# A spectral filter and a feed-forward block on one core: contiguous PSUM writes in the channel stage, ScalarE interleaving even and odd, an evacuation split by bank, table work and statistics in another order

## The chip, the cores and the metric

The kernel runs on one core of one Trainium2 chip. The metric is the device time of one execution in microseconds (us). Before the change it was 194.46 us, the median of three runs (193.75, 194.46 and 197.01). The engines are called as the profile calls them: PE is TensorE (PEld its weight loads), DVE is VectorE, ACT is ScalarE, POOL is GpSimd and SP is SyncE.

## The reference, cut to what matters

```python
x = A_x                                   # 1 x 2048 x 512, bf16
h = x + _A_ref(_layernorm(x), A_w_r, A_w_i)
h2 = h + _B_ref(_layernorm(h), B_w1, B_b1, B_w2, B_b2)

def _A_ref(x, w_r, w_i):
    X = rfft2(x.astype(float32)) * (w_r + 1j * w_i)     # 2048 x 257 frequencies
    return irfft2(X, s=(2048, 512)).astype(bfloat16)

def _B_ref(x, w1, b1, w2, b2):                          # 512 -> 1792 -> 512
    h = relu(x @ w1 + b1)
    return (h * h) @ w2 + b2
```

## The kernel before, in words

Both transforms are made of matmuls against sine tables. The 2048 rows lie as 128 partitions by 16 groups `g`; the 2048-point transform is split in two factors, and the 512-point transform over the channels is split into even and odd frequencies. The order of every engine's instructions is the order in which the kernel is written: at the end `pin` chains all instructions of an engine (L22 to L31, called in L610). Four stretches follow each other.

**Head.** POOL writes integer angle tables (`idxL` and `fiG` for the channel table GF, `idxK` and `fiE` for the row tables EF), ACT turns them into sines. DVE takes the statistics of each group of x (L195 and L196; the groups 3, 7, 11 and 15 are summed by ACT in L188 and L189), POOL makes 1/sqrt of the variance (L203, L204), DVE normalizes (L208). `stage1(g0)` (L211) multiplies two groups by the small table KF and ACT writes them to `Bt` (L222). PE also transposes EF into EI (L264, L270), which DVE copies out of PSUM (L272).

**Channel and row stages, a loop over eight pairs `pr`.** `stage2(pr)` (L309) is the channel transform: eight matmuls of 128x256 into a PSUM tile `p2`, whose even and odd columns lie interleaved (`r j e`), so that a matmul for one `e` writes every second fp32. ACT copies the tile to `U` in bf16 (L318). `stage3(pr)` (L320) multiplies U by the row table EF (L338 to L341) and ACT copies the result to `AB` (L343). `spectral(pr)` (L355) is DVE work: the butterfly that makes X of the next pair out of AB (L352, L353), the products with the weights (L361, mA and mB), Z (L371, L372) and M (L381, L383), while POOL does the real frequencies (L297 to L304). `stage4(pr)` (L386) is the inverse row transform (L399, L400); ACT copies its tile to `T2` (L408), and for the last pair the copy is cut into three pieces on ACT, DVE and ACT (L404 to L406). The PE order in one turn is stage3(pr+2), stage2(pr+3), stage4(pr-1).

**Boundary.** `s5` multiplies T2 by the inverse channel table GI (L455), ACT copies the odd half (L458), `s5b` adds and subtracts (L464, L465), `s6` is the last small transform plus the residual (L469, L470), `s6b` the statistics of the second layer norm (L474, L475), `rstd` and `norm` finish it (L478, L479, L494), `transp` transposes (L506). For the first chunk of two groups this is written out by hand (L591 to L607), with matmuls on ones (`warm`, L227) between.

**Feed-forward.** Five chunks of groups; `up` (L544, L547, L548) and `down` (L563, L567) of one chunk run with the boundary steps of the next chunk between them (`prep_steps`, L514).

## Time and profile before

| what | value |
|---|---|
| runs | 193.75, 194.46, 197.01 us; median 194.46 |
| the profiled execution's own time | 193.75 us |
| its span in the profile | 192.0 us |
| busy: PE / DVE / ACT / POOL | 166.8 / 129.1 / 97.3 / 57.1 us |
| mean granted clock of PE | 0.982 |

The span is the time from the first to the last recorded instruction; the time of the execution holds 1.75 us more. A busy PE is not a PE at its peak: a matmul of 128x256 counts as busy with 270 to 420 ns though the next one begins 110 or 217 ns after it. The chain of waits follows the end of the program back through what released each step. A group's line has the line number, the engine, the operation, tiles and shapes, the count, then busy us and mean ns, then the idle time just before.

### The profile page before, as it was taken

Reading aid. Unit: us, or ns where it says so; the run is one execution under the profiler, and the core shown is the slowest. Engines: PE = TensorE matmul, PEld = TensorE weight load, DVE = VectorE, ACT = ScalarE, POOL = GpSimd, SP = SyncE. Lnnn points to the kernel's source line nnn. Section 1 sums busy time; section 2 is a strip of 40 time slices with the busy share of each in tenths; the row PEclk is TensorE's granted clock in tenths of the full one; section 3 lists DMA queues with packets and bytes.
Section 4 is the critical chain, followed back from the end, with each engine's and each line's share of the span. In section 5 each row is a group of like instructions: output and inputs, shape, how many; then the busy total and the mean of one; then the engine's idle time right before and its main releaser. Section 6 shows DMA issues by size and latency. Waiting matters only on the chain.

```text
span 192.0 us, 2699 instructions
## 1 busy us (share of the span) xinstructions
PE 166.8 (87%) x946; PEld 91.3 (48%) x946; DVE 129.1 (67%) x308; ACT 97.3 (51%) x152; POOL 57.1 (30%) x117
## 2 busy tenths in 40 slices
PE   6667987799864867889999989999999999999992
PEld 2235754366532426744654344544455444456540
DVE  7899717878876174994699724899445986448421
ACT  3499747476783205723774146771327760338400
POOL 8977614543153012302240202240202422006000
PEclk9979999999999699999999999999999999999999
DMA  6857999600000000000000000000100000010001
GB/s 178 301 103 112 296 372 363 139 3 3 0 2 0 0 0 3 0 0 29 27 3 0 27 27 27 3 0 0 55 27 31 2 0 27 27 60 0 0 29 53
DMA packets 13323, 11.19 MB, mean 58 GB/s; under 512 B 2302, under 2 KB 12158, under 8 KB 13310
## 3 DMA queue, kind: packets, MB, share of 16 engines
q1 hardware_dynamic: 13310, 11.03, 20.0%
q8 instruction: 7, 0.11, 0.3%
q14 instruction: 6, 0.05, 0.1%
HBM read 8.93 MB, written 3.02 MB: 62 GB/s over the span
## 4 chain that ended last, share of the span: by engine, by line
PE 59%; DVE 23%; ACT 9%; POOL 5%; issue 2%; ACTq 0%; POOLq 0%; DVEq 0%
PE ph L544 19%; PE po L563 19%; PE p L315 7%; DVE act L548 4%; ACT U L318 4%; DVE st L474 3%; DVE hs L470 3%; DVE st L195 3%; PE p L455 3%; DVE un L208 2%; PE p L506 2%; DVE R L464 2%; DVE R L465 2%; POOL rs L479 1%; ACT u L491 1%
## 5 line engine op out<-in xcount | busy, mean ns | idle before, releaser
L547 ACT ACTIVATE rl<-ph,b1f 128x384 bf16<-128x384 f32 (+2 forms) x70 | 41.9, 602 | 23.7 <-PE ph L544 22.0
L544 PE MATMUL ph<-UT,W 128*128 128x384 bf16 (+2 forms) x280 | 52.9, 336 | 0.5 <-ACT UT L510 0.5
L563 PE MATMUL po<-W,act 128*128 128x512 bf16 x224 | 50.8, 379 | 0.0
L548 DVE TENSOR_TENSOR act<-rl 128x384 bf16<-128x384 bf16 (+2 forms) x70 | 32.3, 478 | 13.0 <-ACT rl L547 12.7
L544 PEld LDWEIGHTS <-W 128*128 128x128 bf16 x280 | 27.4, 98 | 20.1 <-issue 0.6
L551 POOL TENSOR_TENSOR hb<-hs,b2b 128x512 f32<-128x512 bf16 x16 | 18.4, 1152 | 57.2 <-DVE act L548 57.2
L563 PEld LDWEIGHTS <-act 128*128 128x128 bf16 x224 | 21.6, 98 | 26.9 <-issue 2.7
L567 DVE TENSOR_TENSOR ot<-po,hb 128x512 bf16<-128x512 f32 x16 | 11.0, 689 | 18.4 <-PE po L563 18.4
L491 ACT ACTIVATE u<-hs,nm,rs 128x512 bf16<-128x512 bf16 x6 | 4.7, 808 | 24.5 <-DVE nm L488 24.5
L315 PE MATMUL p<-GF,Bt 128*128 128x256 bf16 x64 | 15.0, 417 | 1.0 <-ACT Bt L222 1.0
L219 PE MATMUL p<-KF,un 128*128 128x256 bf16 x32 | 8.0, 290 | 4.8 <-DVE un L208 4.8
L478 POOL TENSOR_SCALAR rs<-mv 128x3 f32<-128x3 f32 (+2 forms) x5 | 1.2, 239 | 35.3 <-DVE mv L475 35.3
L318 ACT CAST U<-p 128x1024 bf16<-128x1024 f32 x8 | 8.1, 1012 | 6.9 <-PE p L315 6.9
L315 PEld LDWEIGHTS <-Bt 128*128 128x128 bf16 x64 | 8.2, 130 | 6.4 <-ACT Bt L222 1.1
L470 DVE SCALAR_TENSOR_TENSOR hs<-p,xs 128x512 bf16<-128x512 f32 x16 | 10.8, 678 | 0.6 <-PE p L469 0.5
L474 DVE BATCH_NORM_STATS2 st<-hs 128x6 f32<-128x512 bf16 x16 | 11.0, 686 | 0.2
L455 PE MATMUL p<-GI,T 128*128 128x256 bf16 x64 | 10.3, 291 | 0.0
L227 PE MATMUL p<-ones 128*128 128x512 bf16 x25 | 8.7, 497 | 1.4 <-DVE ones L139 1.4
L510 ACT COPY UT<-p 128x768 bf16<-128x768 bf16 (+2 forms) x5 | 4.2, 842 | 10.5 <-PE p L506 10.5
L399 PE MATMUL p<-EI,M 128*128 128x256 bf16 x28 | 6.9, 278 | 2.8 <-DVE M L381 1.9
L469 PE MATMUL p<-R,KI 128*128 128x512 bf16 x16 | 6.1, 380 | 3.4 <-DVE R L465 3.2
L227 PEld LDWEIGHTS <-ones 128*128 128x128 bf16 x43 | 4.8, 116 | 8.7 <-issue 5.1
(134 smaller groups left out, 232.2 us busy)
## 6 DMA issues: line engine op xcount, KB each, us to landing
W<-in_B_w_dram SPq DMA_DIRECT2D x2, 1792.0 KB
out_dram<-ot SPq DMA_DIRECT2D x16, 128.0 KB, 1.8
xs<-in_A_x_dram SPq DMA_DIRECT2D x3, 512.0 KB, 6.5
WB<-Wrev SPq DMA_DIRECT2D x2, 449.8 KB, 6.4
WB<-in_A_w_r_dram SPq DMA_DIRECT2D x1, 514.0 KB, 11.9
WB<-in_A_w_i_dram SPq DMA_DIRECT2D x1, 514.0 KB, 7.2
xs<-in_A_x_dram SPq DMA_DIRECT2D x2, 256.0 KB, 3.5
Wrev<-in_A_w_r_dram SPq DMA_DIRECT2D x1, 449.8 KB
```

What stands on the lines that cost most here:

```text
L227: nc.tensor.matmul(o, lhsT=ones[:, 0:P], rhs=ones[:], start=True, stop=True)
L315: nc.tensor.matmul(puv[:, q, :, e, :], lhsT=Bt[:, 2 * t + e, 2 * pr + q, :], rhs=GFv[:, t, :, e, :], start=(t == 0), stop=(t == 1))
L318: nc.scalar.copy(U[:].rearrange("p q c -> p (q c)"), pu[:])
L455: nc.tensor.matmul(pe[:, 256 * e:256 * e + 256], lhsT=T2[:, g, lt].rearrange("p q s -> p (q s)"), rhs=GI[:, lt, :], start=(r == 0), stop=( ...
L470: nc.vector.scalar_tensor_tensor(hs[:, g, :], py[:], WSC, xs[:, g, :], ALU.mult, ALU.add)
L474: nc.vector.bn_stats(st[:], hs[:, g, :])
L544: nc.tensor.matmul(ph[:, 0:n], lhsT=W1[:, d, bass.ts(f, P)], rhs=UT[:, d, 0:n], start=(d == 0), stop=(d == ND - 1))
L547: nc.scalar.activation(rl[:, 0:n], ph[:, 0:n], ACT.Relu, bias=b1f[:, f:f + 1], scale=1.0)
L548: sq = nc.vector.tensor_tensor(act[:, f, 0:n], rl[:, 0:n], rl[:, 0:n], ALU.mult)
L551: add = nc.gpsimd.tensor_tensor(hb[:, g, :], hs[:, g, :], b2b[:], ALU.add)
L563: nc.tensor.matmul(po[:], lhsT=act[:, f, bass.ts(i, P)], rhs=W2[:, f, :], start=(f == 0), stop=(f == NF - 1))
L567: nc.vector.tensor_tensor(ot[:], po[:], hb[:, g, :], ALU.add)
```

## The change

- The PSUM tile of stage2 has the order `q r e j`: the even columns stand together, then the odd ones, each in runs of 128. The ACT copy to U puts them back in the order `r j e`, writing every second bf16.
- T2 has `lt` outside and `g` inside. stage4 takes its four parts in the order 1, 0, 3, 2 instead of 1, 3, 0, 2, so that the first two lie in the first bank of the tile. The last pair's copy is in two pieces, ACT for the first bank and DVE for the second.
- Table work: the row tables (`idxK`, `fiE`) come first on POOL, those for GF after the second batch's statistics; the negation of EF on DVE and `idxD` on POOL come after stage1.
- Statistics: in the head `bn_aggr` of a group is issued after `bn_stats` of the next. In every chunk the first group's statistics of the second layer norm are taken by ACT (a Copy and a Square pass with accumulators) instead of DVE, and POOL makes the variance out of them with two more small operations.
- Order on PE: the transposes of EF come before stage1(8), and three matmuls on ones ahead of it are gone; four stand after the transposes into `tr2`, five in each turn of the loop from pr = 5 on. At the boundary s5(0) and s5(1) come first, then three on ones; both s5b come ahead of s6(0).

```diff
     def stage2(pr):
         pu = mm_tile("p2")
-        puv = pu[:].rearrange("p (q r j e) -> p q r e j", q=2, r=2, e=2)
+        puv = pu[:].rearrange("p (q r e j) -> p q r e j", q=2, r=2, e=2)
...
-        nc.scalar.copy(U[:].rearrange("p q c -> p (q c)"), pu[:])
+        nc.scalar.copy(U[:].rearrange("p q (r j e) -> p (q r) e j", r=2, e=2),
+                       pu[:].rearrange("p (q r e j) -> p (q r) e j", q=2, r=2, e=2))
...
-        for lt in (1, 3, 0, 2):
+        for lt in (1, 0, 3, 2):
...
-        src = pt[:].rearrange("p (l q g s) -> p g l q s", l=4, q=2, g=G)
+        src = pt[:].rearrange("p (l q g s) -> p l g q s", l=4, q=2, g=G)
         if split:
             nc.scalar.copy(dst[:, 0:2], src[:, 0:2])
-            nc.vector.tensor_copy(dst[:, 2:9], src[:, 2:9])
-            nc.scalar.copy(dst[:, 9:16], src[:, 9:16])
+            nc.vector.tensor_copy(dst[:, 2:4], src[:, 2:4])
...
+        if pr >= 5:
+            warm(mm_tile("idle")[:, 0:512], 5)
...
     def ln1_stats(a, b):
-        for g in range(a, b):
-            if g not in ON_ACT:
-                st = fwd.tile([P, 6], FP32, tag="st", bufs=4, name="st")
+        mine = [g for g in range(a, b) if g not in ON_ACT]
+        sts = {}
+        for k in range(len(mine) + 1):
+            if k < len(mine):
+                g = mine[k]
+                sts[g] = st = fwd.tile([P, 6], FP32, tag="st", bufs=4, name="st")
                 nc.vector.bn_stats(st[:], xs[:, g, :])
-                nc.vector.bn_aggr(mv1[:, g, :], st[:])
+            if k > 0:
+                g = mine[k - 1]
+                nc.vector.bn_aggr(mv1[:, g, :], sts.pop(g)[:])
...
+    def s6b(g, on_act=False):
+        if on_act:
+            for f, sc, k in ((ACT.Copy, 1.0 / D, 0), (ACT.Square, float(D) ** -0.5, 1)):
+                junk = ffn.tile([P, D], BF16, tag="junk", bufs=2, name="junk")
+                nc.scalar.activation(junk[:], hs[:, g, :], f, scale=sc, accum_out=mv2[:, g, k:k + 1])
...
+    def rstd(a, b, on_act=()):
+        for g in on_act:
+            nc.gpsimd.tensor_tensor(nm2[:, g:g + 1], mv2[:, g, 0:1], mv2[:, g, 0:1], ALU.mult)
+            nc.gpsimd.tensor_tensor(mv2[:, g, 1:2], mv2[:, g, 1:2], nm2[:, g:g + 1], ALU.subtract)
...
-            steps.append(lambda g=g: s6b(g))
-        steps.append(lambda: rstd(a, b))
+            steps.append(lambda g=g: s6b(g, g == a))
+        steps.append(lambda: rstd(a, b, (a,)))
...
+    s5(0)
+    s5(1)
     idle = bank("idle", "ph", 3)
     warm(idle[:], 3)
-    s5(0)
-    s5(1)
     s5b(0)
-    warm(idle[:], 2)
+    s5b(1)
     s6(0)
-    s5b(1)
-    s6b(0)
-    warm(idle[:], 2)
+    s6b(0, True)
     s6(1)
     s6b(1)
-    rstd(0, 2)
+    rstd(0, 2, (0,))
     norm(0, False)
-    warm(idle[:], 11)
+    warm(idle[:], 14)
```

The order of instructions moves at three places that matter below. Line numbers of the changed kernel are its own. First POOL in the head, from the small index tables on (`idxL` and `fiG` feed GF, `idxK` and `fiE` feed EF, `rs` is 1/sqrt of the variance). Before:

```order
L147 MEMSET mhalf 128x4
L148 IOTA idxL 128x512
L150 MEMSET idxL 128x1
L172 TENSOR_SCALAR fiG<-idxL,cols 128x257
L173 TENSOR_SCALAR fiG<-idxL,cols 128x255
L172 TENSOR_SCALAR fiG<-idxL,cols 128x257
L173 TENSOR_SCALAR fiG<-idxL,cols 128x255
L175 IOTA idxK 128x1152
L203 TENSOR_SCALAR rs_87<-mv_86 128x2
L204 TENSOR_TENSOR rs_87<-rs_87,mhalf 128x2
```

With the change:

```order
L147 MEMSET mhalf 128x4
L167 IOTA idxK 128x1152
L170 TENSOR_SCALAR fiE_123<-idxK,cols 128x1152
L200 TENSOR_SCALAR rs_87<-mv_86 128x2
L201 TENSOR_TENSOR rs_87<-rs_87,mhalf 128x2
L170 TENSOR_SCALAR fiE_124<-idxK,cols 128x1152
L198 TENSOR_TENSOR nm_88<-mv_86 128x1
```

The second `fiE` now stands right behind the first `rs`, which DVE's first normalization waits for; the four `fiG` have moved behind the `rs` of the groups 4 to 7, which the normalization of these groups waits for.

Second the end of the loop on DVE, with the waits: the last M, the copy of the last stage4 tile to T2 and the first s5b. With the change:

```order
L389 TENSOR_TENSOR M<-Z 128x512 [waits DVE_49,PE_49,Pool_49]
L391 TENSOR_TENSOR M<-Z 128x512
L413 CAST T_69<-p_794 128x32x16 [waits Activation_49]
L473 TENSOR_TENSOR R<-p_825,od 128x256 [waits Activation_49]
L474 TENSOR_TENSOR R<-p_825,od 128x256
```

The copy of the second bank (L413) waits on ACT's semaphore, for the count that ACT's copy of the first bank brings it to; and that ACT copy waits for PE's count after all eight matmuls of the tile. Before, the copy on DVE (L405) waited for ACT in the same way.

Third PE at the boundary, from the last stage4 matmul of the loop (L400, in the changed kernel L408) to the first s5 (L455, now L464). Before:

```order
L400 MATMUL p_775<-EI,M 128x256
L227 LDWEIGHTS ones
L227 MATMUL idle<-ones 128x512 [waits Activation_49]
L227 LDWEIGHTS ones
L227 MATMUL idle<-ones 128x512
L227 LDWEIGHTS ones
L227 MATMUL idle<-ones 128x512
L455 LDWEIGHTS T_69
L455 MATMUL p_805<-GI,T_69 128x256
```

With the change:

```order
L408 MATMUL p_794<-EI,M 128x256
L224 LDWEIGHTS ones
L224 MATMUL idle<-ones 128x512 [waits PE_49]
L224 LDWEIGHTS ones
L224 MATMUL idle<-ones 128x512
L224 LDWEIGHTS ones
L224 MATMUL idle<-ones 128x512
L224 LDWEIGHTS ones
L224 MATMUL idle<-ones 128x512
L224 LDWEIGHTS ones
L224 MATMUL idle<-ones 128x512
L464 LDWEIGHTS T_69 [waits DVE_49,Activation_49]
```

Before, three matmuls on ones stood ahead of the first s5 and waited for ACT's last copy to T2 (L406), because their bank was that tile's. Now five stand there that wait for nothing but PE itself, and the wait for the copies to T2 is on the weight load of s5. Behind the eight matmuls of s5 follow three on ones and then both s6 (L478).

More of the change, by code (lines that the diff above doesn't have):

```diff
@@ L77 @@
     GI = persist.tile([P, 4, 256], BF16, name="GI")
-    T2 = persist.tile([P, G, 4, 16, 8], BF16, name="T2")
+    T2 = persist.tile([P, 4, G, 16, 8], BF16, name="T2")
     fwd = tc.alloc_tile_pool(name="fwd", bufs=1)
@@ L244 @@
     stage1(2, 4)
-    nc.vector.tensor_scalar(EF[:, :, 2, :], EF[:, :, 0, :], -1.0, None, ALU.mult)
     nc.gpsimd.memset(ident[:], 0.0)
@@ L258 @@
     ln1_norm(8, 12)
-    stage1(8, 3)
+    stage1(8)
     stage1(10)
-    tr = mm_tile("ptr", BF16)
-    for j in range(16):
-        nc.tensor.transpose(tr[:, P * j:P * j + P], EF[:, j // 2, j % 2, :], ident[:])
     ln1_norm(12, 16)
```

46 lines of the change are left out of this document (25 added, 21 removed).

## The prediction

> **What bounds the kernel now.** I read the stages first: busy time by stretch, cut where the chain of waits changes its character (columns: stretch, length, then busy us of PE, PEld, DVE, ACT and POOL, granted clock, DMA).
>
> ```profile
> 0.00:24.70 24.70, 17.51 (x109) 10.38 (x110) 21.06 (x59) 17.58 (x29) 18.66 (x49) 0.93 0.79 201
> 24.70:61.60 36.90, 30.26 (x172) 18.29 (x173) 26.15 (x63) 23.55 (x25) 14.29 (x42) 1.00 0.35 109
> 61.60:74.00 12.40, 7.96 (x37) 3.71 (x37) 6.13 (x14) 2.12 (x5) 0.97 (x2) 0.86 0.00 0
> 74.00:192.00 118.00, 111.09 (x630) 58.89 (x629) 75.71 (x172) 54.03 (x94) 23.20 (x24) 1.00 0.06 19
> ```
>
> Head (DVE busiest), loop over pairs (no engine full), boundary (nobody busy), feed-forward (PE 94%). Then the chain of waits through one turn of the loop (start us, us, what):
>
> ```profile
> 42.09 1.74 PE p L315 x8
> 43.91 1.02 ACT U L318
> 44.97 0.38 PE p L338
> ...
> 46.00 1.74 PE p L315 x8
> ```
>
> The turn is a circle PE – ACT – PE: eight matmuls of stage2, their copy to U, stage3 on U, the next stage2. 3.91 us a turn. The groups by shape tell what is odd in it:
>
> ```profile
> L315 PE MATMUL p<-GF,Bt 128*128 128x256 bf16 x64 | 15.0, 417 | 1.0 <-ACT Bt L222 1.0
> L219 PE MATMUL p<-KF,un 128*128 128x256 bf16 x32 | 8.0, 290 | 4.8 <-DVE un L208 4.8
> L318 ACT CAST U<-p 128x1024 bf16<-128x1024 f32 x8 | 8.1, 1012 | 6.9 <-PE p L315 6.9
> L343 ACT CAST AB<-p 128x1024 bf16<-128x1024 f32 x7 | 7.1, 1013 | 3.4 <-PE p L341 3.4
> L121 ACT ACTIVATE GF<-fiG 128x1024 bf16<-128x1024 int16 x1 | 1.0, 1039 | 0.0
> ```
>
> L315 and L219 stream the same 256 columns with new weights each time. L315 writes every second fp32 of PSUM and takes 1.74/8 = 0.217 us from start to start at full clock. L219 writes two runs of 128:
>
> ```profile
> 18.93 0.11 PE p L219
> ```
>
> So the interleaved write costs stage2 twice the time: 0.87 us a turn.
>
> DVE has slack in that circle, but little. Its rows (start, us, tile; the bracket is the wait before):
>
> ```profile
> 30.30 0.69 DVE L361 TENSOR_TENSOR mA<-X,WB 128x1024 bf16<-128x1024 bf16 x1 [0.87 <-ACT X L334]
> ...
> 53.27 0.69 DVE L361 TENSOR_TENSOR mA<-X,WB 128x1024 bf16<-128x1024 bf16 x1
> ...
> 55.54 0.43 DVE L352 TENSOR_TENSOR X<-AB 128x512 bf16<-128x512 bf16 x1 [0.98 <-ACT AB L343]
> ...
> 57.56 0.68 DVE L361 TENSOR_TENSOR mA<-X,WB 128x1024 bf16<-128x1024 bf16 x1
> ...
> 60.14 0.42 DVE L383 TENSOR_TENSOR M<-Z 128x512 bf16<-128x512 bf16 x1
> ```
>
> A turn of DVE is 57.56 − 53.27 = 4.29, less 0.98 of waiting: 3.31 us. That is the next bound.
>
> **Loop: what the change takes.** Stage2 becomes 8 × 0.109 = 0.87. Its copy to U reads runs of 128 and writes every second bf16. No ACT row writes so; the nearest in kind is the sine of GF, which reads every second int16 and takes 1039 ns against 1012 to 1013 of the copies. Low bound 1.01; high bound twice that, 2.02, by what a step of two costs PE's writes to PSUM. I take 1.02, since the row on the same engine is the nearer one. The circle is then 3.91 − 0.87 = 3.04 us, shorter than DVE's 3.31. ACT has three copies a turn (AB, U, T2), 3 × 1.01: also shorter. So DVE sets the turn, and the gain is not 0.87 a turn but about 0.6.
>
> From DVE's first product to its last M is now 60.56 − 30.30 = 30.26 us. Without waits it is 7 × 3.31 + 3.00 (the last turn, from 57.56, without a butterfly) = 26.2: **−4.1**. The start gains more: stage3(0) stands on PE behind both first stage2, 3.5 us. With 1.74 us for the two, it waits for the first U instead: 0.87 + 0.2 (drain and semaphore) + 1.02 = 2.1, about **−1.3**. Loop **−5.4** in all; bounds −6.2 (if the turn is 3.2) and +0.6 (copies at 2.02: a circle of 4.04, seven times 0.13 over 3.91, and −0.3 at the start). What DVE now waits for first if I am wrong is AB (the wait of L352).
>
> **Boundary.** The chain from DVE's last M to the first matmul of the feed-forward:
>
> ```profile
> 61.59 0.28 ACT T L404
> ...
> 61.89 0.64 DVE T L405
> ...
> 62.55 0.54 ACT T L406
> ...
> 63.13 1.44 PE idle L227 x3
> 64.57 0.87 PE p L455 x4
> ...
> 68.57 0.61 DVE st L474
> ...
> 69.38 0.59 DVE hs L470
> ...
> 73.98 1.03 PE ph L544 x8
> PEclk9979999999999699999999999999999999999999
> ```
>
> Copies: three in a row end 2.5 us after M (60.56). In the new order ACT still waits for all eight matmuls and DVE for ACT. Two pieces of 512 elements are by estimate 0.6 (0.54 for 448) and 0.7 (0.64 for 448): 1.3 against 1.5. But the second part of stage4 (lt 0 instead of lt 3) now waits for POOL's real sums, which come after M; by the lead of one part's two matmuls, 0.2, I set that off. I count 0 for the split.
> The three matmuls on ones, 1.44 us, leave the path: **−1.4**. Five others take their place and end, at half of 1.44/3 each at full clock, 1.2 us after stage4, under the 1.3 us of copies; without that cover they would cost 1.2. The clock digit of the 14th slice (62.4 to 67.2) is 6, and s5 ran at 0.87/4 = 0.217 a matmul; with PE kept busy it runs at 0.11: **−0.4**.
> Statistics: the chain holds hs, st and mv twice. Now DVE does R twice, hs twice, one st; ACT takes the first group in the shadow of the second hs. Its cost has rows in the head:
>
> ```profile
> 5.07 0.63 ACT L188 ACTIVATE un<-xs 128x512 bf16<-128x512 bf16 x1 [2.55 <-DMA xs<-in_A_x_dram]
> ...
> 6.35 0.19 ACT L189 ACTIVATION_READ_ACCUMULATOR un<-xs 128x1 f32 x1
> ```
>
> 6.54 − 5.07 = 1.47 us, against hs (0.6), st and mv (0.8) of the second group on DVE: level, so st and mv of the first group, 0.8, go, and R of the second group now fills the time in which s6(0), a matmul of 512 columns (0.38 as in L338), runs; POOL's added subtraction I put at 0.2 behind it. **−1.0**. Boundary **−2.8**, bounds −3.3 and −1.4 (only the matmuls on ones).
>
> **Head.** DVE's rows, and the POOL row that lies over one of them:
>
> ```profile
> 8.46 0.66 DVE L195 BATCH_NORM_STATS2 st<-xs 128x6 f32<-128x512 bf16 x1
> ...
> 9.26 0.66 DVE L195 BATCH_NORM_STATS2 st<-xs 128x6 f32<-128x512 bf16 x1
> ...
> 10.05 1.58 DVE L208 TENSOR_SCALAR un<-xs,mv,rs 128x512 bf16<-128x512 bf16 x2
> 11.55 0.48 DVE L245 TENSOR_SCALAR EF<-EF 128x1152 bf16<-128x1152 bf16 x1
> ...
> 19.82 1.79 DVE L208 TENSOR_SCALAR un<-xs,mv,rs 128x512 bf16<-128x512 bf16 x4 [0.37 <-POOL rs L204]
> ```
> ```profile
> 3.32 0.49 POOL L173 TENSOR_SCALAR fiG<-idxL,cols 128x255 int32<-128x255 int32 x1
> ...
> 8.62 2.55 POOL L178 TENSOR_SCALAR fiE<-idxK,cols 128x1152 int32<-128x1152 int32 x2
> ```
> ```profile
> L208 DVE TENSOR_SCALAR un<-xs,mv,rs x16: 381/408/1260, 7.0 to 21.0; 128x512 bf16<-128x512 bf16 x16
> ```
>
> A statistic with its aggregation costs 0.80 from start to start, and the aggregation has to wait until the 0.66 are through; with another statistic between I take 0.70, for twelve less the last of each batch: −0.8. The negation of EF leaves DVE's path to Bt: −0.4. The normalization at 10.05 took 1.58 for two where 0.75 is usual; its first instruction, 1260 ns, ended when POOL's fiE did. This goes (−0.8) and comes back at two places: the second fiE now starts together with the first normalization (I take +0.6, half of its length), and the four fiG lie over that of the groups 4 to 7 (+0.4, what the row at 19.82 shows, where POOL writes fiI: 1.79 for four against 1.4). Net +0.2. On PE the 16 transposes no longer stand between stage1(10) and stage1(12): from the last normalization (19.82 + 1.79 = 21.6) to stage2(0) (24.7, the cut of the stretches) 3.1 us pass, where the last four matmuls (0.4), drain and semaphores (0.4) and a copy (1.0) need 1.8: −1.3. Stage2(0) now also waits for DVE's negation of EF (0.4) and its copy of the transposes out of PSUM (2048 elements against the negation's 1152; by estimate 0.9 at its rate, 1.2 with PSUM as the source), 1.6 behind the last normalization: just covered, and 0.1 to 0.5 if not. Sum −0.8 − 0.4 + 0.2 − 1.3 = −2.3, of which I take **−2.1**; bounds −3.3 (no overlap with POOL) and 0 (1.2 for fiE and 4 × 0.49 for fiG, each blocking DVE to its end).
> The upper bound is what a rule of the Trainium skill gives, "SBUF — State Buffer", section "Who interferes with whom", by which a DVE copy or tensor_scalar in a two-port mode and POOL exclude each other, and whoever issues first keeps the shared ports for the whole instruction. The 1260 ns instruction agrees; the 1.79 for four, with four POOL instructions beside them, does not go that far.
>
> **Feed-forward.** Per chunk DVE loses 0.8 us and ACT gains 1.47.
>
> ```profile
> 73.90:91.40 17.50, 15.62 (x112) 10.32 (x112) 12.03 (x35) 8.99 (x20) 3.42 (x4) 1.00 0.03 9
> 91.40:115.30 23.90, 22.70 (x136) 12.29 (x134) 17.13 (x41) 11.72 (x21) 4.74 (x5) 1.00 0.05 17
> ```
>
> PE idles 1.9 and 1.2 us in the first two chunks, behind DVE; later PE is full and nothing is to be had. Behind ACT's two passes are queued the relus of the next columns, for which PE's `up` waits with three buffers. I take **−0.4**; bounds −1.5 and +1.5 (one pass uncovered in each of two chunks, less a little).
>
> **Sum**, against the profiled execution's 193.75 us (span 192.0): −5.4 − 2.8 − 2.1 − 0.4 = −10.7, so 183.05. That execution is 0.7 below the median, and the fastest of three; I put little of this on it and predict **183.2 us**, against a median of 194.46 before.
>
> **Rivals.** (1) The loop gets only half: DVE goes on waiting for AB, because ACT's three copies, which fill 3.04 of 3.31 us, queue behind each other and GI's sine once more. For it speaks the 0.98 us in the row quoted, a turn in which that sine stands ahead of AB; against it the 0.27 us of slack that each other turn gains. Then 183.2 + 2.7 = 185.9. Chance 0.18.
> (2) The head gains nothing, because each fiE and fiG blocks a normalization to its end: 183.2 + 2.1 = 185.3. For it the 1260 ns row, against it the row at 19.82, where four POOL instructions beside four normalizations cost only 0.4. Chance 0.12. The rule of the Trainium skill quoted above leads here.
> (3) U at twice the time: loop +0.6 instead of −5.4, 189.2. For it: PE's own writes at a step of two. Chance 0.05.
> (4) Slower: the copy writing every second bf16 is no longer a matter of 1 ns an element. The circle is then 2.02 us plus the copy c, on the path seven times and once at the start: 7 × (2.02 + c − 3.91) + (c − 1.02 − 1.3). It decides from where this is +5.3, what the rest gains: c = 2.6 us. At 3.04, three times the row, it is +8.8 and the time 197.4. Nothing in the trace is that slow at a step of two. Chance 0.03.
> That the split is not a split (DVE waits for ACT) is already in the sum.
>
> **Chances and range.** The forecast, 180.3 to 185.0, has 0.62; (1) and (2) 0.30, (3) 0.05, (4) 0.03. The range 179.6 to 187.5 holds the forecast, (1) and (2), and below it the lower bounds of loop and boundary together. A measurement tells about 2% (3.9 us) from no change, so faster means below 190.6: 0.93, with most of (3); within 2%: 0.04; slower 0.03.
>
> **What would show it.** Right: L325, the new line of L315, from start to start at 0.109 us; U near 1.02 us; DVE without a wait before X from the third pair on, turn 3.2 to 3.4; the first s5 some 2.5 us after the last M; full clock there; stage2(0) near 22.6; the feed-forward near 117.6 us. Wrong: U above 1.2 us, AB waits on DVE over 0.3 us a turn, normalizations above 1 us more than twice, or PE idling more than before in the first chunks.

## The result and the profile after

The changed kernel takes 187.3 us (median of four runs, 187.29 to 187.33) against 195.7 of the kernel before in the same session (four runs, 193.75 to 197.01). The ratio, 0.965 with a 95% interval of 0.962 to 0.968, so faster by 3.5%, is taken over the quicker runs of before (193.75 and 194.46) alone, since 196.89 and 197.01 belong to a slower kind that this kernel shows in every session. Forecast were 183.2 us and a gain of 10.7; in the profiled executions the gain is 6.4 (193.75 to 187.33), and the span falls by 6.5, from 192.0 to 185.5. So the direction is right and 4.2 us of the sum are missing. The time lies outside the forecast's own interval, 180.3 to 185.0, and 0.2 us inside the wider range that took in rivals (1) and (2).

The stages again, cut at the same events (the first stage2, the last M, the first matmul of the feed-forward; columns as before: stretch, length, busy us of PE, PEld, DVE, ACT, POOL, granted clock, DMA):

```profile
0.00:24.20 24.20, 17.19 (x108) 9.87 (x109) 20.99 (x57) 17.80 (x29) 18.68 (x49) 1.00 0.78 194
24.20:56.00 31.80, 25.23 (x177) 16.63 (x180) 26.53 (x66) 25.10 (x24) 14.73 (x42) 1.00 0.44 135
56.00:66.30 10.30, 8.29 (x46) 4.08 (x48) 5.32 (x12) 3.25 (x8) 1.59 (x6) 1.00 0.00 0
66.30:185.50 119.20, 111.07 (x621) 58.88 (x629) 73.13 (x165) 57.49 (x110) 25.16 (x32) 1.00 0.06 18
```

| stretch | before | after | measured | forecast |
|---|---|---|---|---|
| to the first stage2 (24.68, 24.23) | 24.7 | 24.2 | −0.45 | −2.1 |
| to the last M (60.56, 55.98) | 35.9 | 31.75 | −4.1 | −5.4 |
| to the feed-forward's first matmul (73.98, 66.31) | 13.4 | 10.3 | −3.1 | −2.8 |
| to the end | 118.0 | 119.2 | +1.2 | −0.4 |

**The loop.** The groups by shape (busy us, then mean ns of one):

```profile
L325 ACT CAST U<-p 128x1024 bf16<-128x1024 f32 x8 | 10.3, 1307 | 1.1 <-PE p L322 1.1
L322 PE MATMUL p<-GF,Bt 128*128 128x256 bf16 x64 | 8.1, 273 | 0.1
L351 ACT CAST AB<-p 128x1024 bf16<-128x1024 f32 x7 | 7.1, 1014 | 3.4 <-PE p L349 3.3
```

Stage2's group falls from 15.0 us and 417 ns to 8.1 and 273, close to L219 before (290 ns): the contiguous write does what was forecast. But the copy to U, now with a step of two on its write, takes 1307 ns against 1014 of AB's copy beside it. In the chain of waits through one turn (start us, us, what) the two copies stand one behind the other:

```profile
37.85 0.38 PE p L346
38.28 0.38 PE p L348
38.66 0.23 PE p L349
39.04 0.76 ACT AB L351
39.95 1.32 ACT U L325
41.31 0.38 PE p L346
```

41.31 − 37.85 = 3.46 us a turn. Stage3 of one pair, its AB, then the U of the next pair, which stands behind AB on ACT, then the next stage3: that is the circle, 0.24 longer than DVE's own turn (3.22, as the kernels without these waits show further down). DVE waits for AB in the last four of its seven turns with a butterfly, 0.16 to 0.18 us and once 0.64, where the sine of GI stands ahead of AB on ACT (columns: start, us, engine, line; the wait in brackets):

```profile
43.55 0.43 DVE L360 TENSOR_TENSOR X<-AB 128x512 bf16<-128x512 bf16 x1 [0.16 <-ACT AB L351]
...
50.95 0.42 DVE L360 TENSOR_TENSOR X<-AB 128x512 bf16<-128x512 bf16 x1 [0.64 <-ACT AB L351]
```

**The boundary.** The chain after the last M (55.56 + 0.42 = 55.98), and PE's granted clock over the span in 40 slices:

```profile
57.07 0.59 ACT T L412
57.69 0.70 DVE T L413
58.53 0.61 PE p L464 x4
...
61.66 1.34 ACT junk L485 x4
```
```profile
PEclk9999999999999999999999999999999999999998
```

The two copies come one after the other, as forecast; s5 starts 2.55 us behind M (4.01 before) and the slice that showed a 6 is at 9. ACT's sums are now a step of the chain.

**The head.** DVE's rows after, and three of DVE before for the same work:

```profile
2.08 1.12 DVE L157 TENSOR_SCALAR mask<-subc,pF 128x128 bf16<-128x128 int32 x1
...
3.75 1.18 DVE L166 TENSOR_SCALAR KF<-KF 128x128 bf16<-128x128 bf16 x1
4.84 1.27 DVE L190 BATCH_NORM_STATS2 st<-xs 128x6 f32<-128x512 bf16 x2
...
7.50 1.57 DVE L205 TENSOR_SCALAR un<-xs,mv,rs 128x512 bf16<-128x512 bf16 x2 [0.37 <-POOL rs L201]
...
13.73 2.05 DVE L205 TENSOR_SCALAR un<-xs,mv,rs 128x512 bf16<-128x512 bf16 x4
...
18.52 1.38 DVE L205 TENSOR_SCALAR un<-xs,mv,rs 128x512 bf16<-128x512 bf16 x4 [0.67 <-POOL rs L201]
20.51 1.64 DVE L205 TENSOR_SCALAR un<-xs,mv,rs 128x512 bf16<-128x512 bf16 x4 [0.61 <-POOL rs L201]
```
```profile
2.09 0.57 DVE L160 TENSOR_SCALAR mask<-subc,pF 128x128 bf16<-128x128 int32 x1
...
3.44 0.42 DVE L169 TENSOR_SCALAR KF<-KF 128x128 bf16<-128x128 bf16 x1
3.81 0.70 DVE L195 BATCH_NORM_STATS2 st<-xs 128x6 f32<-128x512 bf16 x1
```

And POOL after, at the same times:

```profile
2.01 1.11 POOL L167 IOTA idxK<- 128x1152 int32 x1
3.65 1.23 POOL L170 TENSOR_SCALAR fiE<-idxK,cols 128x1152 int32<-128x1152 int32 x1 [0.53 <-DVE cols L163]
...
17.44 1.04 POOL L201 TENSOR_TENSOR rs<-rs,mhalf 128x4 f32<-128x4 f32 x1
...
19.43 1.05 POOL L201 TENSOR_TENSOR rs<-rs,mhalf 128x4 f32<-128x4 f32 x1
```

Lay the two over each other. The mask, 0.57 before, ends at 3.20, just behind the idxK row (3.12); the sign change of KF, 0.42 before, ends at 4.93, just behind the first fiE (4.88). Before, POOL did shorter pieces there, and the same two instructions ended just behind these: the mask at 2.66 behind idxL (2.59), the sign change at 3.86 behind a fiG (3.81). The first statistic is 1.03 us later for it, before any of the forecast's gains begins. At the end DVE waits twice for rs, 0.67 and 0.61, with its statistics long done: POOL, which now has idxL and the four fiG ahead of these rs, has become the head's bound.

**The feed-forward.** ACT, DVE and PE in the first chunk (three answers of the timeline):

```profile
72.15 0.62 ACT L485 ACTIVATE junk<-hs 128x512 bf16<-128x512 bf16 x1
...
73.38 0.46 ACT L564 ACTIVATE rl<-ph,b1f 128x256 bf16<-128x256 f32 x1
```
```profile
73.87 0.29 DVE L565 TENSOR_TENSOR act<-rl 128x256 bf16<-128x256 bf16 x1 [0.86 <-ACT rl L564]
```
```profile
76.69 0.38 PE L478 MATMUL p<-R,KI 128*128 128x512 bf16 x1 [1.12 <-DVE R L474]
```

The relu of 73.38 stands behind both passes over hs; DVE waits 0.86 for it, and R of the chunk's last group, behind that on DVE, keeps PE waiting 1.12. The second chunk starts 0.84 us later after the feed-forward's first matmul than before, the end comes 1.2 later.

### The profile page after: what moved, and what is told of

It is laid out like the page before. It is cut to its first block, busy times and chain, and to the rows that moved or that the text cites. A ratio compares the mean times of both kernels' runs of the same rounds, so it can differ in the third digit from the quotient of the medians.

```text
span 185.5 us, 2755 instructions
## 1 busy us (share of the span) xinstructions
PE 161.8 (87%) x952; PEld 89.5 (48%) x966; DVE 126.0 (68%) x298; ACT 103.6 (56%) x171; POOL 60.2 (32%) x127
## 4 chain that ended last, share of the span: by engine, by line
PE 52%; DVE 18%; ACT 17%; POOL 7%; issue 4%; ACTq 0%; POOLq 0%; DVEq 0%
PE ph L561 21%; PE po L580 20%; ACT U L325 5%; DVE act L565 3%; ACT AB L351 3%; PE p L464 3%; DVE hs L479 2%; ACT rl L564 2%; PE p L523 2%; DVE st L488 2%; POOL rs L201 2%; ACT junk L485 1%; POOL rs L496 1%; PE p L478 1%; DVE R L473 1%
## 5 line engine op out<-in xcount | busy, mean ns | idle before, releaser
L580 PE MATMUL po<-W,act 128*128 128x512 bf16 x217 | 49.9, 379 | 0.4
L325 ACT CAST U<-p 128x1024 bf16<-128x1024 f32 x8 | 10.3, 1307 | 1.1 <-PE p L322 1.1
L224 PEld LDWEIGHTS <-ones 128*128 128x128 bf16 x63 | 6.5, 106 | 8.2 <-issue 2.8
L464 PE MATMUL p<-GI,T 128*128 128x256 bf16 x64 | 9.4, 272 | 0.4 <-DVE T L413 0.4
L351 ACT CAST AB<-p 128x1024 bf16<-128x1024 f32 x7 | 7.1, 1014 | 3.4 <-PE p L349 3.3
L224 PE MATMUL p<-ones 128*128 128x512 bf16 x21 | 7.7, 522 | 1.4 <-DVE ones L139 1.4
L224 PE MATMUL idle<-ones 128*128 128x512 bf16 x36 | 8.9, 379 | 0.1
L478 PE MATMUL p<-R,KI 128*128 128x512 bf16 x16 | 6.1, 380 | 3.2 <-DVE R L474 3.1
L205 DVE TENSOR_SCALAR un<-xs,mv,rs 128x512 bf16<-128x512 bf16 x16 | 7.3, 515 | 1.6 <-POOL rs L201 1.6
L322 PE MATMUL p<-GF,Bt 128*128 128x256 bf16 x64 | 8.1, 273 | 0.1
L219 ACT CAST Bt<-p 128x1024 bf16<-128x1024 f32 x8 | 7.7, 1007 | 0.8 <-PE p L217 0.8
```

Of the source, the lines that this page charges most:

```text
L224: nc.tensor.matmul(o, lhsT=ones[:, 0:P], rhs=ones[:], start=True, stop=True)
L322: nc.tensor.matmul(puv[:, q, :, e, :], lhsT=Bt[:, 2 * t + e, 2 * pr + q, :], rhs=GFv[:, t, :, e, :], start=(t == 0), stop=(t == 1))
L325: nc.scalar.copy(U[:].rearrange("p q (r j e) -> p (q r) e j", r=2, e=2), pu[:].rearrange("p (q r e j) -> p (q r) e j", q=2, r=2, e=2))
L351: nc.scalar.copy(AB[:].rearrange("p u r c -> p (u r c)"), px[:])
L464: nc.tensor.matmul(pe[:, 256 * e:256 * e + 256], lhsT=T2[:, lt, g].rearrange("p q s -> p (q s)"), rhs=GI[:, lt, :], start=(r == 0), stop=( ...
L580: nc.tensor.matmul(po[:], lhsT=act[:, f, bass.ts(i, P)], rhs=W2[:, f, :], start=(f == 0), stop=(f == NF - 1))
```

## The experiments

All times are medians; the changed kernel's 187.3 is the base. The experiments ran on other chips than that base; the lowest run of the kernel before lies between 193.67 and 193.85 on all of them, so sessions differ by up to 0.2 us. The first ten undo or alter one thing each.

**Feed-forward statistics back on DVE.**

```diff
-            steps.append(lambda g=g: s6b(g, g == a))
-        steps.append(lambda: rstd(a, b, (a,)))
+            steps.append(lambda g=g: s6b(g))
+        steps.append(lambda: rstd(a, b))
```

> The changed kernel with one part undone: the statistics of the first group of each feed-forward chunk go back from ACT to DVE; those of the boundary stay on ACT. Theory A (ACT's two passes stand ahead of relus that PE waits for, and this is why the feed-forward takes 119.2 us from its first matmul instead of 118.0): the stretch from the first up matmul to the end returns to about 118.0, the time falls by 1.2, from 187.3 to 186.1. Rival B (the passes are covered and the longer stretch comes from elsewhere, for instance from the order of the weights' last DMA or the state at its start): no change, 187.3, and the stretch stays at 119.2. Rival C (the DVE work given back costs what the forecast said it gains, 0.4): 187.7.

Measured: 186.03 us (186.03 to 186.05), −1.27. The first matmul of the feed-forward stays at 66.32 and the span ends at 184.3: 118.0 us, as before. Theory A. The edit cost what it was thought to hide.

**The channel stage as before.**

```diff
-        puv = pu[:].rearrange("p (q r e j) -> p q r e j", q=2, r=2, e=2)
+        puv = pu[:].rearrange("p (q r j e) -> p q r e j", q=2, r=2, e=2)
-        nc.scalar.copy(U[:].rearrange("p q (r j e) -> p (q r) e j", r=2, e=2),
-                       pu[:].rearrange("p (q r e j) -> p (q r) e j", q=2, r=2, e=2))
+        nc.scalar.copy(U[:].rearrange("p q c -> p (q c)"), pu[:])
```

> The changed kernel with the channel stage as before: stage2 writes every second word of PSUM and ACT copies U straight through; all else as changed. Theory A (the loop's share of the gain, 4.1 us in the traces, comes from this part alone): the turn goes back to 3.9 us, the first product of the loop starts 1 us later, the time is 187.3 + 4.1 = 191.4. Rival B (the warm matmuls, the order of stage4's parts or the table work moved out of the way carry part of it): the turn stays between 3.5 and 3.8 and the time between 188.5 and 190.5.

Measured: 191.41 us (191.40 to 191.44), +4.1. Theory A to the tenth: the loop's gain comes from this part alone.

**U without the interleave, and with the interleave on the other side.** The first keeps the contiguous write to PSUM and copies U straight through. The second gives the same U by the same copy, with j and e exchanged in both patterns, so that ACT jumps in PSUM and writes U in one run.

```diff
-        nc.scalar.copy(U[:].rearrange("p q (r j e) -> p (q r) e j", r=2, e=2),
-                       pu[:].rearrange("p (q r e j) -> p (q r) e j", q=2, r=2, e=2))
+        nc.scalar.copy(U[:].rearrange("p q (r j e) -> p (q r) j e", r=2, e=2),
+                       pu[:].rearrange("p (q r e j) -> p (q r) j e", q=2, r=2, e=2))
```

> The changed kernel without the interleave: stage2 writes PSUM in runs of 128 and ACT copies U straight through, so the columns of U stand in the wrong order. It leaves out the interleave and nothing else, all later work is of the same shapes. Theory A (the write at every second bf16 is what makes the copy take 1.31 us instead of 1.01, and this alone makes the turn 3.46 instead of 3.31, since stage3 waits for AB and then for U on ACT): U takes 1.01, the turn is DVE's 3.31, the loop 7 x 0.15 = 1.0 us shorter and its start 0.3 earlier: 187.3 - 1.3 = 186.0. Rival B (the copy is slow because it follows AB closely or because of the way in which it reads PSUM): U stays at 1.3 and the time at 187.3. Rival C (U falls to 1.01 but the turn stays at 3.4 to 3.5 because DVE's own work takes so long now): 186.9.

> The changed kernel with the interleave on the other side of the same copy: ACT walks PSUM in the order j, e (every next word 128 words away) and writes U in one run. The result is the same. Theory A (ACT pays for the step of two on its write; a jump on the read of PSUM is free): U takes 1.01 and the time is as without the interleave, 186.0. Rival B (the innermost run of two on the read side costs more than the step on the write side): U takes 1.5 to 2 us, the turn 3.6 to 4.1, the time 188.5 to 192.

Measured: 185.20 us without the interleave (three runs 185.16 to 185.20, one 190.97) and 185.18 with it on the read side (185.18 to 185.20). In the second kernel the group of the copy and DVE's row:

```profile
L325 ACT CAST U<-p 128x1024 bf16<-128x1024 f32 x8 | 8.0, 1017 | 1.1 <-PE p L322 1.1
```
```profile
41.13 0.68 DVE L369 TENSOR_TENSOR mA<-X,WB 128x1024 bf16<-128x1024 bf16 x1
...
44.34 0.68 DVE L369 TENSOR_TENSOR mA<-X,WB 128x1024 bf16<-128x1024 bf16 x1
```

Theory A in both: the jump on the read of PSUM costs nothing (1017 ns, as much as the copy without the interleave), the step of two on the write of U costs 0.29 us. The turn becomes 3.21 and DVE has no wait left in it. The gain of 2.1 is more than the 1.3 expected, because DVE's own turn is 3.21 and not the 3.31 of the forecast: without a wait each instruction starts some 0.08 us before the one ahead has ended, and subtracting the wait in brackets leaves this out. The run of 190.97 comes back with the four edits below.

**The head as before, with all else changed** (the text of the head, from the first constants to the last index table, taken over from the kernel before).

> The changed kernel with the whole head (tables, statistics, normalizations, stage1) in the order of before; channel stage, boundary and feed-forward as changed. Theory A (as the two traces read: the reordered head is worth only 0.45 us, since POOL's integer work now lies on DVE's instructions): stage2 starts 0.45 later, at 24.7, the time is 187.3 + 0.45 = 187.75. Rival B (the forecast's 2.1 us are there, but something else in the changed kernel takes them back later): 189.4. Rival C (the reordered head is worse than the old one once the channel stage is quick, because GF or the second half of EI comes later): 187.0 or less.

Measured: 187.85 us (187.84 to 188.80), +0.55. Stage2 starts at 24.78. Theory A: the whole reordering of the head is worth half a microsecond; nothing of it is lost later.

**The sign change of KF on ACT.**

```diff
-    nc.vector.tensor_scalar(KF[:, P:2 * P], KF[:, 0:P], -1.0, None, ALU.mult)
+    nc.scalar.mul(KF[:, P:2 * P], KF[:, 0:P], -1.0)
```

> The changed kernel with one instruction moved from DVE to ACT: the sign change of KF, which on DVE takes 1.18 us beside POOL's first fiE and 0.42 where POOL runs shorter pieces; ACT has nothing to do between 2.5 and 4.9 us. Theory A (POOL's long instruction holds DVE's two-byte tensor_scalar until it ends, and this pushes all of the head): the first statistic starts at 3.9 instead of 4.84, stage2 0.9 earlier, the time 186.4. Rival B (from the fifth us on POOL's own chain bounds the head, not DVE's start): the first normalization comes earlier, stage2 does not by more than 0.2, the time 187.1 to 187.3. Rival C (it is not POOL that holds the instruction: ACT takes as long): 187.3 or more.

```profile
3.75 0.31 ACT L166 ACTIVATE KF<-KF 128x128 bf16<-128x128 bf16 x1 [1.24 <-DVE KF L165]
```

Measured: 186.24 us (186.18 to 186.28), −1.06. ACT does in 0.31 us, beside the same fiE on POOL, what takes DVE 1.18; the first statistic starts at 3.70. Theory A: the instruction is long because POOL works beside it, and the whole head hangs on it.

**POOL's index row for fiG ahead of rs.**

```diff
     table_e(0)
+    nc.gpsimd.iota(idxL[:].rearrange("p (r e j) -> p r e j", r=2, e=2), pattern=[[0, 2], [1, 2], [2, 128]], base=0,
+                   channel_multiplier=0)
+    nc.gpsimd.memset(idxL[:, 256:257], 256)
     ln1_sums(3)
...
     ln1_stats(8, 12)
-    nc.gpsimd.iota(idxL[:].rearrange("p (r e j) -> p r e j", r=2, e=2), pattern=[[0, 2], [1, 2], [2, 128]], base=0,
-                   channel_multiplier=0)
-    nc.gpsimd.memset(idxL[:, 256:257], 256)
```

> The changed kernel with POOL's index row for fiG (0.58 and 0.12 us) issued behind the first fiE, where POOL has nothing to do for 1.5 us, instead of ahead of the fiG. Theory A (POOL's queue is what the last two batches of normalizations wait for, 0.67 and 0.61 us): rs comes 0.7 to 0.8 earlier, the batch of groups 8 to 11 starts at 17.9, that of 12 to 15 at 19.8, the time 186.6. Rival B (those waits are for ACT's sums or DVE's own statistics, which then end last): 187.1 to 187.3.

Measured: 186.66 us (186.65 to 186.67), −0.64. The last two batches start at 17.89 and 19.88, 0.63 earlier. Theory A: POOL's queue ends the head.

**The boundary's statistics back on DVE; the matmuls on ones out of the loop.**

```diff
-    s6b(0, True)
+    s6b(0)
-    rstd(0, 2, (0,))
+    rstd(0, 2)
```

> The changed kernel with the statistics of the boundary's first group back on DVE (those of the feed-forward chunks stay on ACT). Theory A (the statistic and its aggregation, 0.8 us, go back on the path to the first up matmul, less the 0.1 by which ACT's sums and POOL's subtraction end last now): 187.3 + 0.7 = 188.0. Rival B (the second group's chain decides either way, and POOL's subtractions eat the gain): 187.3 to 187.5. The forecast had counted 1.0 for this step.

```diff
-        if pr >= 5:
-            warm(mm_tile("idle")[:, 0:512], 5)
```

> The changed kernel without the matmuls on ones in the last three turns of the loop and ahead of s5. Theory A (they keep PE's granted clock up over the copies of the last pair): the clock falls in the boundary, the eight matmuls of s5 take 0.2 instead of 0.11 each, the time 187.7 to 188. Rival B (the clock stays up through 1.4 us without a matmul): 187.3. Rival C (they stand in the way of stage4): 187.0.

Measured: 188.16 us (188.12 to 188.18), +0.86, for the statistics: theory A, and near the forecast's 1.0. Without the matmuls on ones 189.05 us (188.00 to 189.11): theory A in kind, and more than expected. The profiled execution took 188.0, and in it

```profile
58.43 1.87 PE L462 MATMUL p<-GI,T 128*128 128x256 bf16 x8 [1.40 <-DVE T L413]
```

s5 takes 1.87 us instead of 1.03, after PE has stood still twice, for 1.20 and for 1.40 us; the granted clock from 58.4 to 60.4 is 0.50, where the changed kernel has 1.00. The three other runs took one more microsecond at mean granted clocks of 0.962 to 0.973, where the profiled one had 0.982; there is no trace of these, so where that microsecond goes stays open.

**Two PSUM tiles for the last pair.** The forecast took the split for no split, because DVE's copy waits for ACT's. Does it have to?

```diff
         pt = mm_tile("p4")
+        pt2 = mm_tile("p4b") if split else pt
...
-                o = pt[:, 256 * lt:256 * lt + 256]
+                o = (pt2 if lt > 1 else pt)[:, 256 * lt:256 * lt + 256]
...
-            nc.vector.tensor_copy(dst[:, 2:4], src[:, 2:4])
+            src2 = pt2[:].rearrange("p (l q g s) -> p l g q s", l=4, q=2, g=G)
+            nc.vector.tensor_copy(dst[:, 2:4], src2[:, 2:4])
```

> The changed kernel with stage4 of the last pair writing two PSUM tiles instead of one, the first for ACT's copy, the second for DVE's. Theory A (DVE's copy waits for ACT's only because both read one tile): the two copies run side by side, 0.59 beside 0.69 us, s5 starts 0.6 earlier, the time 186.7. Rival B (the order is kept by T2, into which both write, or the first s5 needs something else as late): 187.3.

```profile
57.07 0.69 DVE L415 CAST T<-p4b 128x512 bf16<-128x512 f32 x1 [1.09 <-PE p4b L409]
```
```profile
56.87 1.24 PE L224 MATMUL idle<-ones 128*128 128x512 bf16 x5
58.17 1.03 PE L466 MATMUL p<-GI,T 128*128 128x256 bf16 x8
```

Measured: 187.06 us (186.99 to 187.07), −0.25, little more than sessions differ by, so the reading rests on the trace. DVE's copy starts 0.62 earlier, behind PE and no longer behind ACT (theory A), but s5 starts only 0.36 earlier: it has no wait at all before it, the five matmuls on ones fill PE until then. Work that a wait covered sets the start when the wait goes.

**Four edits together.** U's copy on the read side, the feed-forward statistics on DVE, KF's sign on ACT, the early index row; and the same with the two tiles.

> The changed kernel with four of the edits tried by themselves: the interleave on the read side of U's copy, the feed-forward's statistics on DVE, the sign change of KF on ACT, the index row of fiG behind the first fiE. Theory A (the four causes lie one behind the other in time and add): 187.3 - 2.1 - 1.3 - 1.1 - 0.6 = 182.2, what the forecast without its three errors would have been near. Rival B (the two of the head share POOL's gap of 1.5 us, which shrinks to 0.4 when the statistics start earlier): 182.5 to 182.8.

> The same four edits and the two PSUM tiles of the last pair. Theory A (the copies run side by side): 0.6 below the version with four, 181.6. Rival B (they don't): as the version with four.

Measured: 187.15 us (186.94 to 187.66) and 186.73 (186.82, 186.63, 188.36 and once 182.18). Neither theory: single gains of 5.1 us add up to 0.2, yet one run in eight is where the sum says. The trace of the four edits: POOL, then DVE beside it.

```profile
46.48 0.23 POOL L438 MEMSET GI<- 1x128 bf16 x1
46.64 3.97 POOL L439 CAST b1f<-b1b 128x14 f32<-128x14 bf16 x1
50.58 0.19 POOL L304 TENSOR_TENSOR ta<-SD,AB 128x4 f32<-128x4 f32 x1
```
```profile
46.66 0.68 DVE L369 TENSOR_TENSOR mB<-X,WB 128x1024 bf16<-128x1024 bf16 x1
...
49.88 0.68 DVE L369 TENSOR_TENSOR mB<-X,WB 128x1024 bf16<-128x1024 bf16 x1
50.59 0.46 DVE L379 TENSOR_TENSOR Z<-mA,mB 128x512 bf16<-128x512 bf16 x1
...
52.99 0.43 DVE L389 TENSOR_TENSOR M<-Z 128x512 bf16<-128x512 bf16 x1 [1.61 <-PE p L408]
```

The head and the turns are as good as hoped (stage2 at 22.71, turn 3.22). Then a copy of 14 numbers a partition takes 3.97 us on POOL; in the changed kernel it took 0.19. Behind it stand the real products and sums, and behind these, on PE, stage4 of the last three pairs with five matmuls on ones after each. PE stands still for 3.85 us, and from there the chain of waits runs through PE alone up to the last copies of T2 (start us, us, what):

```profile
52.90 2.13 PE idle L224 x5
...
55.97 1.08 PE idle L224 x5
```

Against the same edits without a hold (182.35, further down) this costs 4.8 us, and 3.2 of the path are these ten matmuls on ones, the first five at twice their length (granted clock 0.52 from 51.5 to 55.0). The copy ends at 50.61, 0.05 us after DVE's last mB (50.56), and that is the first place since 46 at which a DVE instruction does not begin before the one ahead of it has ended. In the changed kernel DVE waits for AB in these turns, and the copy (50.38) fell into such a wait (50.32 to 50.95). An arrival inside an unbroken run need not be held, though: with the interleave on the read side DVE has no pause either, all four of its runs are at 185.2, and in the trace POOL gets in at the next change of instruction:

```profile
48.17 0.73 POOL L439 CAST b1f<-b1b 128x14 f32<-128x14 bf16 x1
```

(The one run of 190.97 without the interleave would fit a hold; it has no trace.)

**The bias copy elsewhere.** Three kernels with the four edits: the copy on ACT, at the same place (`nc.scalar.copy(b1f[:], b1b[:])`); the copy on POOL but behind the last pair (`if pr == 7:`); this one with the two tiles and three instead of five matmuls on ones in the last turn.

> The four edits, and the copy of the bias to fp32 on ACT instead of POOL, at the same place (behind the sine of GI). Theory A (DVE's instructions, end to end without a gap, shut POOL's copy out until DVE pauses): ACT's copy runs at once at 46.3 in 0.2 to 0.3 us, the real sums are on time, and the time is 182.2, the sum of the four gains. Rival B (the copy waits for its DMA, which lands near 50.5): ACT stands still as POOL did, AB and T2 come late, 186 or more. Rival C (another POOL instruction is shut out in its place, the real products or sums): 185 to 187.

> The four edits, and the copy of the bias on POOL behind the last pair's real sums, where DVE pauses for stage4. Theory A (POOL is shut out only while DVE runs without a gap): the copy takes 0.19 us, the time 182.2 in every run. Rival B (POOL's copy is slow wherever it stands the first time it runs, for its code): 4 us again, in the shadow of the boundary, since the first relu needs the bias only 10 us later: also 182.2, but with a copy of 4 us in the trace.

> The four edits, the copy of the bias late, two PSUM tiles for the last pair, and three instead of five matmuls on ones ahead of s5 (with two tiles the five end at 58.1, after the copies at 57.8, and s5 waits for them). Theory A: 182.2 less 0.25 for the two tiles as measured and less up to 0.4 for the two matmuls: 181.6. Rival B (with fewer matmuls on ones the clock falls as in the kernel without them): 182.5 or more.

Measured: on ACT four runs of 182.44 to 182.70 and three of 187.22 to 187.82; late on POOL two of 182.4 and four of 186.91 to 188.78; with all repairs two of 181.85 and four of 186.38 to 187.24. The sum of the gains is there, in some of the runs. In the others, as far as there are traces (one of the first kernel, one of the third), it is rival C of the first: POOL's next instruction takes the place of the copy. With the copy on ACT:

```profile
46.69 4.32 POOL L304 TENSOR_TENSOR ta<-SD,AB 128x4 f32<-128x4 f32 x1
```
```profile
50.26 0.69 DVE L369 TENSOR_TENSOR mB<-X,WB 128x1024 bf16<-128x1024 bf16 x1
```

Again the end (51.01) lies 0.06 behind the end of DVE's last mB (50.95). So it is neither the copy nor its data; it is whatever POOL issues behind the two rows of GI. These wait for ACT's sine of GI, and so POOL arrives in the middle of a DVE run without a pause. The trace of the late copy is of a run of 182.39: there the products arrive at 46.68, also in the middle, and take 0.74.

**No arrival in the middle; a pause on DVE.** Two kernels take away the arrival: GI's two rows and the copy of the bias go behind the last pair's real sums, in the version with four edits and in the one with all repairs. A third leaves POOL's order alone and lets DVE pause once a turn, by moving the next pair's butterfly behind the two Z, so that Z has to wait for mB.

```diff
         if pr == 4:
             sin_of(GI[:].rearrange("p t c -> p (t c)"), fiI[:])
+        if pr == 7:
             nc.gpsimd.memset(GI[0:1, 2, 0::2], 1.0)
             nc.gpsimd.memset(GI[0:1, 2, 1::2], -1.0)
             nc.gpsimd.tensor_copy(b1f[:], b1b[:])
```
```diff
-        nxt[0]()
         nc.vector.tensor_tensor(Z[:, :, 0], mA[:, :, 0], mB[:, :, 1], ALU.subtract)
         nc.vector.tensor_tensor(Z[:, :, 1], mA[:, :, 1], mB[:, :, 0], ALU.add)
+        nxt[0]()
```

> The four edits, with POOL's two settings of GI's row and the copy of the bias behind the last pair's real sums, so that POOL never stands waiting for ACT's sine of GI and its real products come right behind the real sums, as in the other turns. Theory A (POOL is shut out only when it arrives in the middle of DVE's unbroken run; behind the M that it waits for it gets in): no POOL instruction of the loop over 0.8 us, 182.4 in every run. Rival B (POOL can be shut out anywhere in the unbroken run, by chance): some runs at 186 or more again.

> The same with two PSUM tiles for the last pair and three instead of five matmuls on ones ahead of s5. Theory A: 0.55 below the kernel with the four edits and the late rows, 181.85, in every run. Rival B (shut out by chance): some runs at 186 or more.

> The four edits, POOL's order as in the kernel with the four edits, but on DVE the next pair's first butterfly behind the two Z instead of ahead of them, so that Z waits for mB to drain in every turn, as it does in the last turn, where POOL got in. Theory A (a pause of a few hundredths on DVE lets POOL in): POOL's copy is held at most to the end of the turn's mB, under 1 us, or to the next turn's, under 3.5; with the pause itself at about 0.05 to 0.1 a turn the time is 182.5 to 183.2 in every run. Rival B (the hold has nothing to do with DVE's pauses): about 4 us again in some runs, 186.9.

Measured: 182.35 us (182.33 to 182.43, five runs), 181.94 (181.77 to 182.47, six runs), 183.34 (183.25 to 183.64, five runs). No run of the sixteen is held up. In the first, POOL's products at the place of the hold, and in the third the copy of the bias:

```profile
46.75 0.65 POOL L304 TENSOR_TENSOR ta<-SD,AB 128x4 f32<-128x4 f32 x1
```
```profile
46.64 0.39 POOL L439 CAST b1f<-b1b 128x14 f32<-128x14 bf16 x1
```

Theory A in the first two. The third is free of holds too, as theory A said, a little above its 182.5 to 183.2: the pause makes the turn 3.34 to 3.36 instead of 3.22, and that is its price of one microsecond. But it does not show that the pause is what let POOL in: the copy got in at the end of an M (46.97), before the turn's pause came. That DVE's pause ends a hold fits all four traces with a hold (four edits, the same with two tiles, copy on ACT, all repairs), which end 0.05 to 0.06 us behind the mB ahead of the first pause; the pause is at the same place in all of them, so it was not tried elsewhere. What decides whether POOL gets in at an ordinary change from one DVE instruction to the next stays open.

The version with all repairs is the fastest: 181.94 us, ratio to the kernel before 0.938 (0.935 to 0.940), 2.9% below the changed kernel.

## Why the prediction was wrong, point by point

**Loop, −5.4, measured −4.1: the copy to U was mis-sized.** The step was "Low bound 1.01; high bound twice that", and the choice of 1.02 "since the row on the same engine is the nearer one". It took 1.307. The row was on the right engine, but a sine that reads with a step, and the change writes with one. The jump on the read side of the same copy is free (1017 ns), and the row's 1039 spoke of reads only; the step on the write side is not free. With it the second half failed: AB's wait, 0.16 to 0.64, stayed. This is what rival (1) described, DVE still waiting for AB because ACT's copies queue behind each other; it came at half of the rival's 2.7 us, and by the longer U, for with U at 1.017 no wait is left. The circle in the forecast (stage2, U, stage3) also left out that U stands behind AB on ACT; with U at 1.02 it is still shorter than DVE's turn. All else of this part held: L322 at 0.109 us, the start of the loop −1.05 with the long copy and −1.33 with the short one (4.29 us from stage2 to the first product, 5.62 before) for a forecast of −1.3, and DVE as the next bound. Its turn was 3.22 rather than 3.31; with the short copy the stretch from stage2 to the last M is 29.5 us, −6.3.

**Head, −2.1, measured −0.45: the "net +0.2" of POOL beside DVE was +2.** The other three terms came near: three statistics with their aggregations take 2.07 us from start to start instead of 2.40, about −1.2 in all (forecast −0.8); the negation of EF −0.4 (−0.4); from the last normalization to stage2 2.1 instead of 3.1 us (−1.0 for −1.3). But of POOL only the normalizations were looked at (+0.8, −0.9 and +0.6, forecast +0.6, −0.8 and +0.4). Not looked at were two small DVE instructions that meet idxK and the first fiE (+1.03), and POOL's own queue, which the moved fiG lengthens ahead of the last two rs (0.67 and 0.61 of waiting instead of 0 and 0.37); 0.3 less of waiting ahead of the first normalization and 0.15 less in the last one are to be set against this. The 0.31 us on ACT and the early index row show both. Rival (2), by which the head gains nothing, came near in size; of its mechanism, POOL's blocking, the forecast had searched the large instructions only. The rule that stood beside it (the Trainium skill, "SBUF — State Buffer", section "Who interferes with whom") agrees with the two early rows, 1.12 and 1.18 us, which end 0.08 and 0.05 behind POOL's.

**Boundary, −2.8, measured −3.1: right.** s5 2.55 us behind M (−1.46 for −1.4), the rest −1.6 for −1.4. Taken alone, the statistics are worth 0.86 of the 1.0, and the matmuls on ones at least 0.7, more than the 0.4 for the clock. That the split is none was right, and so was the warning that without the cover the five matmuls would cost time: with two tiles it was that cover which went.

**Feed-forward, −0.4, measured +1.2: wrong in sign, within the bounds of ±1.5.** The forecast named what was queued behind the two passes and then counted the relief on DVE. But PE's waits there are for DVE by way of ACT: the square needs the relu. The step that failed is counting DVE's 0.8 a chunk as a gain and ACT's 1.47 as covered; undoing the edit gives 1.27 back.

**Sum.** Missed: 1.3 in the loop, 1.65 in the head, 1.6 in the feed-forward, less 0.3 in the boundary, 4.25 of 10.7. The four edits that repair these three misses bring 182.35 us, below the forecast of 183.2, once POOL is kept out of DVE's way in the loop. That the sum then comes out is in part luck: DVE's shorter turn adds 0.9 to the loop that the forecast had not counted. The hold was in no rival; in the trace of the changed kernel POOL's copy falls into one of the waits for AB, and that its loop was spared for this reason is an inference from that one trace.

## What to carry to other kernels

Price a strided access by side: look for a row that strides on the same side, read or write, and where there is none, try the permutation on the other side of the same copy. When an edit moves work to another engine, list what is queued behind it there and what each of the two engines does at that moment, small instructions too; a relief on the engine that waits last is no gain when the work lands on the engine it waits for. And when the last wait of a loop goes, look at who lived in that wait: PE's filler, and POOL's few numbers, had their place there.

## What the runs showed of the hardware

- ACT, 1024 elements a partition from fp32 PSUM to bf16 SBUF: 1017 ns straight through, 1017 ns with the read going to and fro between two runs 128 words apart, 1307 ns with a write at every second element.
- POOL and DVE in turn: a 128x128 tensor_scalar of DVE takes 1.18 us beside a POOL instruction of 1.23 us, 0.42 beside one of 0.49, and ends 0.05 behind POOL's in both; on ACT it is 0.31 at the same moment. The other way round, POOL instructions that take 0.2 us where DVE pauses took 3.97 to 4.32 in four traces in which they arrived inside an unbroken run of DVE's two-input bf16 instructions, through nine changes from one to the next, and ended 0.05 to 0.06 behind the instruction ahead of the first pause. In four other traces they arrived inside such a run and took 0.39 to 0.74. The rule of the Trainium skill ("SBUF — State Buffer", section "Who interferes with whom") is about one instruction, for which whoever issues first keeps the shared ports; here POOL was held over nine changes in a row.
- The same kernel can show both: 182.4 and 187.3 us in one session (copy on ACT). Of the traces, those of such kernels at 182.4 us have no hold, and those at 186.4 to 187.3 have one.
